# Another order of 950 TensorE units in a talking-heads attention with a squared-ReLU layer behind it

## The chip, the cores and the metric

One core of a Trainium2 chip runs the whole program. The metric is the device time of one execution in microseconds (us), less is better. Engines: TensorE (PE, with its weight loads PEld), VectorE (DVE), ScalarE (ACT), GpSimd (POOL) and SyncE (SP); the last two issue nearly all transfers.

## What is computed

Attention over 8 batches of 12 heads, 448 positions and 64 columns, in which the heads are mixed by two 12 x 12 matrices: once before the softmax and once after. Behind it comes a layer with 2048 hidden columns.

```python
scores = scale * np.matmul(q, k.transpose(0, 1, 3, 2))
scores = np.einsum('bhij,hg->bgij', scores, w_pre)
scores = scores - np.max(scores, axis=-1, keepdims=True)
attn = np.exp(scores)
attn = attn / (np.sum(attn, axis=-1, keepdims=True) + 1e-09)
attn = np.einsum('bhij,hg->bgij', attn, w_post)
return np.matmul(attn, v).astype(np.float32)
...
x = np.ascontiguousarray(attn_out.transpose(0, 2, 1, 3)).reshape(B * S, H * D)
h = np.maximum(x @ w_in, 0.0)
return (h * h @ w_out).astype(np.float32)
```

Inputs and output are float32; the kernel multiplies in bfloat16.

## The kernel before, in words

The kernel does not loop on the chip. Python code writes out one long program: it first records tasks (one engine, one function that emits instructions, the tasks it depends on), then a planner class, `_Plan`, puts them in an order for each engine, and then `emit_engine` (line 1405) emits each engine's tasks in that order, with semaphore waits for what they depend on. Each engine works strictly in its order, so whatever stands first and waits holds up all that is behind it.

A batch goes through these stages. TensorE's work is cut into *units*, each some 2 to 28 matmuls, and each kind of unit is a stream (the digit in brackets):

- **transposes** [0] (`emit_T`, line 711; matmuls at lines 731 and 735): q and k of a third of the heads, loaded by POOL into `qraw` and `kraw` (`load_qk`, 598), are transposed and copied into `qkt`. There are 6 units a batch, q and k for each third of the heads.
- **QK** [1] (`emit_QK`, 867; line 884): scores of a tile of up to 128 positions, copied by ACT or DVE into one half of `stage` (lines 450 and 451). A half is written again two tiles later.
- **ring moves** (`emit_rel`, 923): SP moves the scores from `stage` into the ring `dring` of 16 slots, so that 10 positions of all 12 heads (a *chunk*, 45 a batch) lie on the partitions of one slot. A slot is filled again when the pre unit 16 chunks earlier has read it.
- **pre** [2] (`emit_pre`, 945; line 953): two chunks of scores times the first mixing matrix. For each chunk ACT then takes the exponential, with the row sums (an *exp*, line 970), DVE the reciprocal (984), and POOL multiplies the second mixing matrix by it (a *fold*, 991).
- **direct** [5] (`emit_direct`, 822; line 832): in batch 0 alone the first 22 chunks are computed without `stage` and ring, from q scaled by the mixing weights.
- **post** [3] (`emit_post`, 1005; line 1023): 16 small matmuls that mix the heads of two chunks and transpose them; copied into `a2t`. A `pring` slot serves again 10 chunks later.
- **AV** [4] (`emit_AV`, 1066; line 1082): attention times v, copied into `xt`; two halves a batch.
- **F1** [6, 7] (`emit_F1`, 1118; lines 1128 and 1149): the first matrix of the layer, then ReLU (ACT or DVE, 1180 and 1181) and square (DVE, 1190) into `h2t`.
- **F2** [8, 9] (`emit_F2`, 1249; lines 1269 and, at the very end, 1218): the second matrix; results are copied to `osb` and sent out by POOL.

A unit writes into one or two of the 8 PSUM banks. It can begin only when the copies of an earlier unit out of these banks are done; these copies, called evacuations here, run on ACT or DVE, whichever the planner expects to finish earlier. Units come in four tilings of the array (full, two rows, two columns, quarters).

The order of TensorE's units is no result of the planner. It is written out by hand as a string of 950 digits, `ORDER` (line 28): each digit takes the next unit of that stream. All other engines' orders follow from it: the planner walks through the string with built-in estimates of each task's duration, of transfers and of instruction loading (in blocks of `BLOCK` = 256 instructions), and appends at each step the task that can start first. Tasks of loads and ring moves are so placed among POOL's folds and SP's queue. At the start of the program, up to `WARM`, it also fills expected idle time of TensorE with matmuls on dummy data (`warm_up`, 560; line 572).

```python
t = self.streams[int(order[at])][0]
if t.nwait:
    return None
est = max(self.free[PE], t.avail)
...
per_engine, committed = plan.run(ORDER)
```

Of the kernel before, what the change touches and what calls it, by code (L numbers as in the profile page):

```python
# [25 lines left out]
DMA_END = {"move": 2800.0, "load": 2300.0}  # L26
INF = float("inf")
ORDER = (
    "0000115551100515551555555555511555555531155333555555511355555555553335550022555533320000"
    "2434112411116333366622727737321622267711367373363111244422266663117723377613372166611227"  # L30
    "7722009333921193922380202821833830021441114218133822382183317613167222177633166336222444"
    "2236731267331761376111702028366228338338311777722002441226666333377220071811381118222893"
    "1193319131922291933392244344229163316220071173362216173337362216721761002637337002288111"
    "8331822291913393319222444223833181138113822244423161162273373163161227373202062263731736"
    "1163720027200291191139311932283281138133822244422391191339233922244422383383181138116331"
    "6020276227263721177337336216600226371172200933911191339222818111831382228183338324444224"
    "4228363161200733763226171171633622276376733372200441118822383182002931193319119223922293"
    "1913833831813811922244442216736227161367336117163372276221673373391229129393822283833382"
    "2244438222836883367676336736764447676766787877667667677879989988988999"
)  # L40


# [1418 lines left out]
```

## Time and profile before

| what | value |
|---|---|
| median of 3 runs | 526.93 us (525.52 to 529.73) |
| the profiled execution: time | 527.09 us |
| the profiled execution: span from first to last instruction | 525.3 us |
| TensorE busy | 514.3 us, 98% |
| ACT busy | 426.7 us, 81% |
| DVE busy | 394.1 us, 75% |
| POOL busy | 198.0 us, 38% |
| transfers issued by software queue q0, by q1 | 32.81 MB, 37.32 MB |
| read from HBM, written | 45.70 MB, 11.01 MB |

How to read it: busy time of TensorE counts a matmul from its start to a modelled end, and neighbours overlap, so 98% does not say that 2% is all that is lost. In the lists below a line such as `DVE stage L451` names an engine, the tile it writes and the line of the kernel; `x28` is a count of instructions. In a list of waits, the engine that waited stands left of the arrow, what ended the wait right of it; then total us, times, and the longest in us.

### The profile page before, as it was taken

How to read it: one execution, taken by the hardware profiler on the slowest of the kernel's cores; microseconds unless marked ns; L12 is line 12 of the kernel's file. 1: busy time of each engine (PE TensorE's matmuls, PEld its weight loads, DVE VectorE, ACT ScalarE, POOL GpSimd, SP SyncE). 2: the span in 40 equal slices, each digit the busy share in tenths (PEclk: the TensorE clock that was granted, in tenths of full speed). 3: DMA queues.
4: the chain of work that ended last, by engine and by line, in shares of the span. 5: the costliest groups of instructions: out<-in, count | busy, mean ns of one | idle time of the engine just before them, and what ended most of it. 6: DMA issues, size and time to landing. Idle time of an engine off the chain costs nothing.

```text
span 525.3 us, 23159 instructions
## 1 busy us (share of the span) xinstructions
PE 514.3 (98%) x9636; PEld 325.9 (62%) x9636; DVE 394.1 (75%) x987; ACT 426.7 (81%) x1221; POOL 198.0 (38%) x391
## 2 busy tenths in 40 slices
PE   8998999999999999999999999999999999999997
PEld 3455677567776564566547664577555665467874
DVE  8946988789979668878887787975788768865330
ACT  3879999889989889888998888988889877886321
POOL 9703445424641364134633456024632232242000
PEclk9999999999999999999999999999999999999999
DMA  8999999746984589636984699437963567541003
GB/s 160 204 216 181 170 170 189 182 105 143 179 168 87 128 173 183 138 75 154 177 167 93 150 180 181 102 71 153 198 122 82 124 142 131 114 105 45 3 20 101
DMA packets 82172, 71.79 MB, mean 137 GB/s; under 512 B 13222, under 2 KB 79446, under 8 KB 82070
## 3 DMA queue, kind: packets, MB, share of 16 engines
q0 software_dynamic: 36624, 32.81, 38.6%
q1 hardware_dynamic: 45158, 37.32, 29.3%
q8 instruction: 77, 1.26, 1.0%
q10 hardware_dynamic: 288, 0.20, 0.1%
q14 instruction: 25, 0.20, 0.1%
HBM read 45.70 MB, written 11.01 MB: 108 GB/s over the span
## 4 chain that ended last, share of the span: by engine, by line
PE 88%; DVE 4%; ACT 4%; DMA 2%; issue 1%; POOL 0%; DVEq 0%
PE ps L1269 26%; PE ps L1149 17%; PE ps L1023 8%; PE ps L953 7%; PE ps L1082 7%; PE ps L1128 7%; PE ps L884 6%; PE ps L832 5%; PE ps L1218 2%; PE ps L735 2%; ACT pring L970 2%; DMA dring<-stage 2%; ACT stage L450 1%; DVE stage L451 1%; PE ps L731 1%
## 5 line engine op out<-in xcount | busy, mean ns | idle before, releaser
L970 ACT ACTIVATE pring<-ps 128x448 bf16<-128x448 f32 x360 | 191.0, 555 | 14.3 <-PE ps L953 8.3
L1269 PE MATMUL ps<-w_out_sb,h2t 64*128 64x384 bf16 x1664 | 152.0, 323 | 0.1
L991 POOL TENSOR_TENSOR wk2s<-wk2b,rinv 128x120 bf16<-128x120 bf16 (+1 forms) x179 | 69.3, 392 | 210.8 <-DVE rinv L984 210.2
L451 DVE CAST a2t<-ps 128x480 bf16<-128x480 f32 (+1 forms) x194 | 118.1, 638 | 17.4 <-PE ps L1023 16.0
L1149 PE MATMUL ps<-xt,w_in_sb 64*128 64x448 bf16 (+2 forms) x1344 | 121.8, 323 | 0.2
L451 DVE CAST stage<-ps 128x448 bf16<-128x448 f32 (+1 forms) x174 | 104.3, 617 | 12.9 <-PE ps L884 10.0
L1269 PEld LDWEIGHTS ps<-w_out_sb,h2t 64*128 64x128 bf16 x1664 | 79.7, 94 | 49.8 <-issue 3.6
L450 ACT ACTIVATE stage<-ps 128x448 bf16<-128x448 f32 (+1 forms) x186 | 96.4, 557 | 17.2 <-PE ps L884 16.4
L450 ACT ACTIVATE a2t<-ps 128x480 bf16<-128x480 f32 (+1 forms) x174 | 92.3, 580 | 13.4 <-PE ps L1023 13.0
L1149 PEld LDWEIGHTS ps<-xt,w_in_sb 64*128 64x128 bf16 x1344 | 61.2, 94 | 41.2 <-PE ps L953 2.5
L970 ACT ACTIVATION_READ_ACCUMULATOR pring<-ps 128x1 f32 x360 | 79.4, 221 | 0.0
L1301 POOL DMA_DIRECT2D out_dram<-osb x52 | 33.6, 652 | 103.2 <-ACT pring L970 47.4
L1023 PEld LDWEIGHTS ps<-wk2s,pring 60*128 60x128 bf16 x2880 | 55.7, 93 | 23.7 <-issue 4.2
L1023 PE MATMUL ps<-wk2s,pring 60*128 60x60 bf16 x2880 | 61.7, 187 | 2.0 <-issue 0.9
L1190 DVE TENSOR_TENSOR h2t<-h1t 128x448 bf16<-128x448 bf16 (+2 forms) x176 | 52.6, 327 | 8.4 <-ACT h1t L1180 7.9
L984 DVE RECIPROCAL rinv<-rowsum 128x2 f32<-128x2 f32 (+1 forms) x184 | 28.9, 157 | 38.1 <-ACT pring L970 37.8
L1180 ACT ACTIVATE h1t<-ps 128x448 bf16<-128x448 f32 (+2 forms) x85 | 38.7, 462 | 20.0 <-PE ps L1149 16.8
L953 PE MATMUL ps<-dring,wk 60*64 60x448 bf16 (+1 forms) x676 | 52.2, 363 | 0.8 <-ACT pring L970 0.6
L1181 DVE TENSOR_SCALAR h1t<-ps 128x448 bf16<-128x448 f32 (+2 forms) x91 | 43.3, 485 | 11.9 <-PE ps L1149 7.8
L884 PE MATMUL ps<-qkt 64*128 64x448 bf16 (+1 forms) x360 | 49.2, 353 | 1.0 <-DVE h1t L1181 0.8
L1128 PE MATMUL ps<-xt,w_in_sb 128*128 128x228 bf16 (+1 forms) x384 | 42.2, 260 | 0.0
L1082 PE MATMUL ps<-a2t,vraw 128*64 128x220 bf16 (+1 forms) x768 | 40.7, 260 | 0.0
(57 smaller groups left out, 422.6 us busy)
## 6 DMA issues: line engine op xcount, KB each, us to landing
dring<-stage SPq DMA_DIRECT2D x309, 105.0 KB
out_dram<-osb POOLq DMA_DIRECT2D x52, 192.0 KB, 4.1
qraw<-in_q_dram POOLq DMA_DIRECT2D x42, 112.0 KB, 5.3
kraw<-in_k_dram POOLq DMA_DIRECT2D x42, 112.0 KB, 5.3
w_in_sb<-in_moe_w_in_dram POOLq DMA_DIRECT2D x8, 384.0 KB, 16.6
vraw<-in_v_dram POOLq DMA_DIRECT2D x24, 128.0 KB
w_out_sb<-in_moe_w_out_dram POOLq DMA_DIRECT2D x8, 384.0 KB, 8.4
vraw<-in_v_dram POOLq DMA_DIRECT2D x24, 96.0 KB
```

The costliest lines, as they stand in the source:

```text
L450: return eng.activation(o, i_, AF.Copy)
L451: return eng.tensor_copy(o, i_)
L884: r_ = eng.matmul(ps[y * w:(y + 1) * w, g.banks[x], 0:S], qkt[r0:r0 + 64, pb, p + y, 0, i0:i0 + w], qkt[r0:r0 + 64, pb, p + y, 1, :], star ...
L953: r_ = eng.matmul(ps[64 * y:64 * y + 64, gr.banks[x], 0:S], wk1[64 * x:64 * x + 64 - R0 * x, :], dring[64 * x:64 * x + 64 - R0 * x, (g0 + ...
L970: return eng.activation(pring[:, pr, 0:S], ps[:, gr.banks[x], 0:S], AF.Exp, accum_out=rowsum[:, pr, :])
L991: return eng.tensor_tensor(wk2s[:, p0:p0 + n, :], i0.to_broadcast([128, n, PR]), rinv[:, p0:p0 + n, :].to_broadcast([128, n, PR]), ALU.mult)
L1023: r_ = eng.matmul(ps[:, gr.banks[x], o0:o0 + PR], pring[64 * x:64 * x + PR, pr + y, j0:j0 + 2 * PJ], wk2s[64 * x:64 * x + PR, pr + y, :], ...
L1082: r_ = eng.matmul(ps[kk * 64:kk * 64 + 64, g.banks[0], x * n:(x + 1) * n], vraw[:, h, s, :], a2t[half][:, s, h, a0:a0 + n], start=(s == 0) ...
L1128: r_ = eng.matmul(ps[:, g.banks[0], 0:n], w_in_sb[:, ft, t * 128:(t + 1) * 128], xt[:, ft, c0:c1], start=(ft == 0), stop=(ft == NFT - 1))
L1149: r_ = eng.matmul(ps[:, g.banks[x], 0:n], w_in_sb[64 * y:64 * y + 64, ft, t * 128:(t + 1) * 128], xt[64 * y:64 * y + 64, ft, c0:c1], start ...
L1190: return eng.tensor_tensor(h2t[:, t16, o0:o0 + n], h1t[:, s, 0:n], h1t[:, s, 0:n], ALU.mult)
L1269: r_ = eng.matmul(ps[:, g.banks[hh], 0:FH], h2t[64 * y:64 * y + 64, t16, col:col + 128], w_out_sb[64 * y:64 * y + 64, t16, hh * FH:(hh + 1 ...
```

## The change

The string `ORDER` is replaced by another of the same length with the same count of each digit (48 zeros, 159 ones, 173 twos, 184 threes, 48 fours, 50 fives, 88 sixes and sevens, 64 eights, 48 nines). The new one is from a search that began at large steps in its first third and was cooled over the whole. Within a stream the units keep their order; how the streams interleave is new from the third digit on. All orders of the other engines that the planner derives are made anew with it, and so is which of ACT and DVE does an evacuation. No function is changed.

```diff
 ORDER = (
-    "0000115551100515551555555555511555555531155333555555511355555555553335550022555533320000"
-    "2434112411116333366622727737321622267711367373363111244422266663117723377613372166611227"
...
-    "1913833831813811922244442216736227161367336117163372276221673373391229129393822283833382"
-    "2244438222836883367676336736764447676766787877667667677879989988988999"
+    "0011005551150055551551555555555555555330055555111555555513355533155331552255555531333002"
+    "4310022434111663372217667223376262233773613177631114214422367672266733326731177112671136"
...
+    "1193393381833811182224442237631611736131617222763363622267127733739311922939222883338338"
+    "2224442228383383676768676776337674447676776767686866776978989988988999"
 )
```

In the two built programs each engine issues the same kinds of instructions: TensorE 9636 matmuls in both, in 956 and 957 units with the warm-ups (6 and 7 of them, 20 matmuls in both). The tiling changes 267 times between neighbouring units before and 269 times after. ACT's tasks go from 861 to 851, DVE's from 979 to 989. Batch 1's first two transposes (the seventh and eighth zero) come between the two halves of chunk 9's direct scores instead of behind those of chunk 19. SP's queue has the same order in both.

More of the change, by code (lines that the diff above doesn't have):

```diff
@@ L28 @@
 ORDER = (
-    "0000115551100515551555555555511555555531155333555555511355555555553335550022555533320000"
-    "2434112411116333366622727737321622267711367373363111244422266663117723377613372166611227"
[L31 to L37, printed above, removed]
-    "1913833831813811922244442216736227161367336117163372276221673373391229129393822283833382"
-    "2244438222836883367676336736764447676766787877667667677879989988988999"
+    "0011005551150055551551555555555555555330055555111555555513355533155331552255555531333002"
+    "4310022434111663372217667223376262233773613177631114214422367672266733326731177112671136"
+    "6702209323920209339121838122833820021441114218123833383118326112772226667133176333722442"
+    "2671336611142003772238316613627228338338122777620103442176633722002676711181318133822289"
+    "3319311931192224913392244422991161363371373611620027237362216721376100262733372020811813"
+    "3831182229193319313922244422381381118333822244422163361371237316116222737200263363372137"
+    "6211672007022091191339113922381183118133822244422293193319333922244314128318221836181363"
+    "3722762216730027336216712007363226171372200911931193319222838331811382228118333822444224"
+    "4431831613600271172267316376122673337371002763362244412288311820208239313922191193392229"
+    "1193393381833811182224442237631611736131617222763363622267127733739311922939222883338338"
+    "2224442228383383676768676776337674447676776767686866776978989988988999"
 )
```

## The prediction

> **What bounds the kernel now.** I read the head of the profile first, then the chain that ended last, then TensorE's waits, and last the timeline and the chain around its longest pauses.
>
> ```profile
> span 525.3 us, 23159 instructions
> PE 514.3 (98%) x9636; PEld 325.9 (62%) x9636; DVE 394.1 (75%) x987; ACT 426.7 (81%) x1221; POOL 198.0 (38%) x391
> PEclk9999999999999999999999999999999999999999
> ...
> PE 88%; DVE 4%; ACT 4%; DMA 2%; issue 1%; POOL 0%; DVEq 0%
> ```
>
> TensorE bounds: 98% busy, 88% of the chain, full clock in all slices. ACT and DVE, which empty PSUM, are at 81% and 75% and can hold it up in places. All that a new order can change is the pauses of TensorE. Busy time hides most of them (ends of matmuls are modelled), so I took steps: from the first matmul of a unit to the first matmul of the next. In the trace these are almost constant for one kind of unit. The lower quartile of each kind, in us: F2 1.30, F1 of 448 columns 1.14, AV 0.75 to 0.78, direct scores 0.57 or 0.38, transposes 0.22, post 0.22, pre and QK 0.19. A unit with a change of tiling behind it takes 0.09 to 0.10 more (F2 1.39, F1 1.23, post 0.32, pre 0.29).
>
> Summed over the 956 units, changes included: warm-up 8.6, transposes 13.6, QK 33.6, direct 25.8, post 42.8, pre 39.6, AV 38.8, F1 151.3, F2 148.2: 502.3 us. Measured from the first matmul to the last unit's end, the same stretch is 520.2. So **17.9 us are pauses**: 15 over 0.2 us make 7.2, 26 of 0.1 to 0.2 make 3.9, the rest are small. The five longest that have one cause show in the waits and pieces of the chain:
>
> ```profile
> PE ps L1023 <- issue: 0.9, 1, 0.9
> PE ps L884 <- DVE h1t L1181: 0.8, 1, 0.8
> PE ps L735 <- issue: 0.8, 1, 0.8
> PE ps L953 <- ACT pring L970: 0.6, 1, 0.6
> PE ps L1023 <- ACT stage L450: 0.5, 1, 0.5
> ```
>
> ```profile
> 47.51 0.43 PE L735 MATMUL ps<-ident,kraw 64*64 64x64 bf16 x28
> 47.82 0.41 PE L735 MATMUL ps<-ident,qraw 64*64 64x64 bf16 x28
> ...
> 50.77 0.37 PE L1023 MATMUL ps<-wk2s,pring 60*128 60x60 bf16 x14 [0.93 <-issue]
> ```
>
> ```profile
> 207.73 0.63 DVE stage L451
> ...
> 208.37 0.63 DVE stage L451
> ...
> 209.07 0.53 DVE stage L451
> ...
> 209.63 0.64 DVE h1t L1181
> ```
>
> Two are "issue" in the middle of a unit, after many tiny matmuls in a row (0.93 at 50 us; 0.75 at 373 us inside transposes). No semaphore is waited for there. The instruction queue q8 makes 77 transfers of 16 KB, each 0.9 to 1.8 long; TensorE's 19,272 matmuls and weight loads and some 960 waits over 77 is about 256 each, the planner's BLOCK. So I read these two as instructions that came late. The other three are surges of evacuations, as in the last fence: one engine works off four copies while TensorE has no free bank.
>
> **The change part by part.** Only the digits of ORDER differ. Side by side, both built kernels have 9636 matmuls and the same 950 units.
>
> *Steps without pauses.* Changes of tiling go from 267 to 269, warm-up matmuls stay 20 (in 7 runs, not 6). With the same steps the new order sums to 502.8: **+0.4**. One answer; nothing hides it, TensorE is the chain.
>
> *Surges.* I ran along each order with the steps above and kept a sum of evacuation asked for: 0.52 for an exp, 0.42 to 0.56 for copies, with 2 us of ACT and DVE taken off per us. In the old order, units at a sum over 2.5 us are 101, and lost some 38 ns each in the mean (0.93 at 50 us left out); units between 1 and 2.5 lost 19 to 24, below 1 us 7. In the new order the units over 2.5 are 81 (over 3.5: 6 for 12; highest 4.4 for 5.2), and 20 more lie below 1 us. Old losses on new counts: **-0.6**. Bounds: the three surges of 0.84, 0.65 and 0.52 gone and none for them, -2.0; as much anew, +2.0. I take -0.6, since the counts fall a little and nothing else does. Ten evacuations move from ACT (861 to 851 tasks) to DVE, the less busy one; they are in the counts.
>
> *Instructions.* Counted in blocks of 256, the densest block before takes 2.31 us of steps and is followed by the 0.93 pause; in the new order the densest there takes 3.26, because batch 1's first transposes move ahead by 15 us, between direct scores. That is 0.95 longer, as long as the pause: -0.9. What is late next there is a surge (sum 3.7 now, 4.6 before), counted above. The block at 373 us goes from 4.90 to 5.12: -0.2. But new blocks of 4.07 and 4.11 appear where the old ones of 4.22 to 4.35 cost 0 to 0.28: +0.2. **-0.9**; bounds -1.7 (both pauses gone) and +1.7 (two such new ones). [...]
>
> *Loads and the score ring.* POOL keeps its instructions, but its loads of q and k stand elsewhere among its folds, which wait for ACT and DVE. A place is the sum of the steps up to a unit; lead is the place of the transpose less the end of the last unit that anything ahead in POOL's queue waits for. The shortest before was 8.0 (batch 4, last k), then 9.2, and TensorE never lost 0.1 to one load after the start. Now it is 7.6 (batch 3, first k), 8.5, 8.9, 9.0 and 9.3.
>
> ```profile
> DMA to landing us min/median/max: 3.4/5.4/11.9
> ```
>
> At the median all are in time; at the maximum the first would cost 4.3. On SP's queue the moves of scores into the ring go out one per 0.8 to 1.2 us. Counted by 0.85 each and 4.2 to land, the tightest use of a ring slot has 2.1 us left (0.7 before), the tightest reuse of a stage half 1.9 (batch 7; 2.3 before). So **+0.4** for one load a little late; bounds 0 and +4.3. There are no gains here, since nothing here costs much now.
>
> *Post close behind pre.* The least way from a pre to its post grows tighter: 8 posts under 2.8 us, 2 before; 2.15 the shortest for 2.48. Behind lie two exps (2 x 0.52 and 0.22), a reciprocal of 0.16 and a fold of 0.39, some 1.9 with hand-overs. The old ones under 2.8 lost 0.01. **+0.2**; bounds 0 and 8 x 0.1.
>
> *The end.* Both orders end in the same 12 F2 units, so the last 5 us stay: 0.
>
> Sum: 0.4 - 0.6 - 0.9 + 0.4 + 0.2 = -0.5. The profiled execution took 527.1 (span 525.3 and 1.8 around it), 0.2 above the median of the runs, 526.9. So 526.6 for such an execution, **526.4** as a median.
>
> **Rivals.**
>
> *No different.* The planner sees neither late instructions nor late landings truly, so pauses might come back elsewhere: 17.9 again, 527.1 + 0.4 = 527.5 profiled, 527.3 as median. For it: surges of 3.1 us and more are 19 for 20 before. Against: the one block of 2.31 is gone for certain.
>
> *Slower: late loads.* Two or more of the five leads of 7.6 to 9.3 meet landings near 11.9. Transposes stand in TensorE's order, so all behind them waits. At the maximum the five cost 4.3 + 3.4 + 3.0 + 2.9 + 2.6; two of them 6 to 7.7: 533. It decides from a landing 9 us after the lead's start on. For it: landings at 78 to 102 us and 187 to 217 us run beside ring moves. Against: the old leads of 8.0 and 9.2 held.
>
> *Faster.* The surges and stalls over 0.2 us (7.2 us) go and none come: 526.9 + 0.4 - 7.2 = 520.1. For it: the highest sum falls by 0.8 us. Against: the number of surges hardly falls, and each order has its own.
>
> **How the numbers follow.** Forecast 0.50, no different 0.30, slower 0.11, faster 0.09. A measurement of this kernel can tell about 1% from no change (521.7 to 532.2): the first two cases lie within it, the others beyond. The forecast's own terms reach from 526.9 + 0.4 - 2.0 - 1.7 = 523.6 to 526.9 + 0.4 + 2.0 + 1.7 = 531.0 without a late load. The faster case lies half in; so the range is 521.8 to 531.0, with 0.1 above and 0.1 below left out. Faster 0.09, same 0.80, slower 0.11.
>
> **What would show it.** Right: no "issue" pause of over 0.5 us at TensorE near 50 us; TensorE's steps again sum to about 503; its pauses to 16 to 18. Surges: the waits of TensorE for ACT and DVE total less. Loads: no wait of line 735 for a transfer. Wrong: a wait for a transfer at batch 2 to 5's transposes (lines 735), or a pause of over 2 us at any one place.

## The result, and the profile after

| | before | changed |
|---|---|---|
| median of 20 runs each | 526.78 us (524.68 to 531.76) | 531.36 us (527.25 to 537.42) |
| the profiled execution: time, span | 527.1, 525.3 us | 531.7, 529.8 us |
| TensorE's steps | 502.3 us | 502.8 us |
| TensorE's pauses | 17.8 us | 21.9 us |

The ratio is 1.0062 (95% interval 1.0037 to 1.0088): some 3.3 us slower (4.6 by the medians), where a gain of 0.5 had been worked out. Runs over 1.5% above the fastest of their kernel are left out of the ratios as disturbed: 537.42 here, and in the experiments one run each of e3, e8 and e9, three of the twelve of e10 (531.55 to 532.44; with all runs counted its mean lies at 1.0010) and four of the kernel before.

The head of the profile and the engine line of the chain, which answer to the first lines shown of before:

```profile
span 529.8 us, 23188 instructions
PE 515.2 (97%) x9636; PEld 323.2 (61%) x9636; DVE 400.0 (76%) x997; ACT 421.6 (80%) x1211; POOL 198.5 (37%) x391
PEclk8999998999999999999999999999999999999999
...
PE 85%; DMA 5%; DVE 4%; ACT 3%; issue 1%; POOL 0%; SPq 0%; DVEq 0%; ACTq 0%
```

Busy times are nearly as before, but transfers went from 2% of the chain to 5%, and the granted clock fell below full speed in slices 1 and 7. What TensorE waited for (us in total, times, longest):

```profile
PE ps L735 <- issue: 2.5, 1, 2.5
PE ps L953 <- DMA dring<-stage: 1.9, 1, 1.9
...
PE ps L1023 <- POOL wk2s L991: 0.7, 2, 0.5
PE ps L735 <- DMA kraw<-in_k_dram: 0.5, 1, 0.5
```

Two lines are new in kind: TensorE waits for a move of scores into the ring (L953 is pre), and a little for a load of k. The pause of 0.93 at 50 us in a post is gone; at nearly the same place one of 2.49 stands in batch 1's transposes (start, duration, engine, line, idle before it):

```profile
51.93 0.41 PE L735 MATMUL ps<-ident,qraw 64*64 64x64 bf16 x28
54.84 0.41 PE L735 MATMUL ps<-ident,kraw 64*64 64x64 bf16 x28 [2.49 <-issue]
```

The chain shows the ring wait from the other side:

```profile
72.83 0.16 SPq L930
...
73.03 10.37 DMA dring<-stage
...
83.44 0.40 PE ps L953 x4
```

The tenth move of batch 1 left SP's queue at 73.0, took 10.4 us to land, and the pre that reads it began the moment it was there. Windows of 3 to 7 us show the clock (the last three columns are granted clock, DMA share and GB/s):

```profile
8.40:15.30 6.90, 6.18 (x89) 2.94 (x82) 6.24 (x18) 2.60 (x5) 6.90 (x13) 0.51 1.24 205
...
80.00:83.50 3.50, 1.14 (x16) 0.64 (x13) 1.19 (x6) 1.98 (x8) 3.31 (x7) 1.00 1.21 221
83.50:87.00 3.50, 3.50 (x22) 2.58 (x22) 1.40 (x6) 1.16 (x4) 0.98 (x2) 0.53 1.08 192
```

TensorE did 1.14 us of work between 80.0 and 83.5, and behind this it ran at half clock for 3.4 us. The same stretches before, at full clock:

```profile
8.40:15.30 6.90, 6.87 (x160) 3.96 (x161) 6.87 (x20) 3.27 (x8) 6.90 (x13) 1.00 1.25 205
...
83.50:87.00 3.50, 3.50 (x40) 2.31 (x38) 3.17 (x11) 3.26 (x10) 1.04 (x3) 1.00 0.94 151
```

Pauses summed by place (sum of the steps up to a unit, in us) say where the 4.0 more came from:

| place | 0–19 | 19–42 | 42–68 | 68–102 | 102–200 | 200–300 | 300–400 | 400 on |
|---|---|---|---|---|---|---|---|---|
| before | 1.05 | 0.22 | 2.84 | 2.10 | 3.85 | 3.25 | 3.67 | 0.86 |
| changed | 3.56 | 0.15 | 3.04 | 5.71 | 2.66 | 3.21 | 2.56 | 0.97 |

2.5 is the half clock at the start, 3.6 is the stretch with the ring wait and the half clock behind it, and 2.3 comes back between 102 and 400 us. One profile can hold accidents, so the experiments had to say which of these belongs to the order.

### The profile page after: what moved, and what is told of

It is laid out like the page before. It is cut to its first block, busy times and chain, and to the rows that moved or that the text cites. A ratio compares the mean times of both kernels' runs of the same rounds, so it can differ in the third digit from the quotient of the medians.

```text
span 529.8 us, 23188 instructions
## 1 busy us (share of the span) xinstructions
PE 515.2 (97%) x9636; PEld 323.2 (61%) x9636; DVE 400.0 (76%) x997; ACT 421.6 (80%) x1211; POOL 198.5 (37%) x391
## 4 chain that ended last, share of the span: by engine, by line
PE 85%; DMA 5%; DVE 4%; ACT 3%; issue 1%; POOL 0%; SPq 0%; DVEq 0%; ACTq 0%
PE ps L1269 25%; PE ps L1149 19%; PE ps L1023 7%; PE ps L953 7%; PE ps L1082 6%; PE ps L884 6%; PE ps L832 5%; PE ps L1128 5%; PE ps L1218 2%; DMA dring<-stage 2%; DMA kraw<-in_k_dram 2%; PE ps L735 2%; ACT pring L970 1%; DMA wall<-in_w_pre_dram 1%; ACT stage L450 1%
## 5 line engine op out<-in xcount | busy, mean ns | idle before, releaser
L451 DVE CAST a2t<-ps 128x480 bf16<-128x480 f32 (+1 forms) x194 | 118.9, 641 | 17.8 <-PE ps L1023 17.1
L451 DVE CAST stage<-ps 128x448 bf16<-128x448 f32 (+1 forms) x183 | 109.5, 617 | 14.5 <-PE ps L884 12.5
L1269 PEld LDWEIGHTS ps<-w_out_sb,h2t 64*128 64x128 bf16 x1664 | 78.2, 94 | 50.6 <-issue 2.2
L450 ACT ACTIVATE stage<-ps 128x448 bf16<-128x448 f32 (+1 forms) x177 | 90.8, 553 | 17.8 <-PE ps L884 17.2
L450 ACT ACTIVATE a2t<-ps 128x480 bf16<-128x480 f32 (+1 forms) x174 | 91.6, 572 | 15.4 <-PE ps L1023 15.0
L1181 DVE TENSOR_SCALAR h1t<-ps 128x448 bf16<-128x448 f32 (+2 forms) x93 | 45.4, 497 | 14.4 <-PE ps L1149 7.8
L953 PE MATMUL ps<-dring,wk 64*64 64x448 bf16 (+1 forms) x676 | 52.3, 361 | 3.0 <-DMA dring<-stage 1.9
L1180 ACT ACTIVATE h1t<-ps 128x448 bf16<-128x448 f32 (+2 forms) x83 | 36.7, 446 | 22.0 <-PE ps L1149 15.3
L884 PE MATMUL ps<-qkt 64*128 64x448 bf16 (+1 forms) x360 | 50.3, 357 | 0.8 <-DVE qkt L451 0.7
L1128 PE MATMUL ps<-xt,w_in_sb 128*128 128x220 bf16 (+1 forms) x384 | 43.5, 266 | 0.0
```

Source lines behind the costliest of these rows:

```text
L450: return eng.activation(o, i_, AF.Copy)
L451: return eng.tensor_copy(o, i_)
L884: r_ = eng.matmul(ps[y * w:(y + 1) * w, g.banks[x], 0:S], qkt[r0:r0 + 64, pb, p + y, 0, i0:i0 + w], qkt[r0:r0 + 64, pb, p + y, 1, :], star ...
L953: r_ = eng.matmul(ps[64 * y:64 * y + 64, gr.banks[x], 0:S], wk1[64 * x:64 * x + 64 - R0 * x, :], dring[64 * x:64 * x + 64 - R0 * x, (g0 + ...
L1128: r_ = eng.matmul(ps[:, g.banks[0], 0:n], w_in_sb[:, ft, t * 128:(t + 1) * 128], xt[:, ft, c0:c1], start=(ft == 0), stop=(ft == NFT - 1))
L1269: r_ = eng.matmul(ps[:, g.banks[hh], 0:FH], h2t[64 * y:64 * y + 64, t16, col:col + 128], w_out_sb[64 * y:64 * y + 64, t16, hh * FH:(hh + 1 ...
```

## The experiments

The theory to test: the ring wait costs the 3 us, and it comes from one digit. The last QK unit of batch 1's first tile stands at digit 108 of the new order and at 99 of the old (counted from 0; by steps, 53.6 against 49.9 us), and SP can begin the moves of this tile only when that unit's scores are copied out. The rivals: the half clock at the start, the pause near 50 us, or the new order behind 102 us. Ratios below are to runs of the kernel before on the same chip; they rest on 6 runs of e3, 9 of e5 and e7, and 12 of each of the others.

**Splices: which stretch holds the loss.** At digits 28, 78, 144 and 216 both orders have used up the same units, so pieces can be exchanged there. They lie at about 19, 42, 68 and 102 us of steps.

```diff
-ORDER = new
+ORDER = old[:28] + new[28:]                    # e1_old_start
+ORDER = new[:78] + old[78:144] + new[144:]     # e2_old_42_68
+ORDER = new[:144] + old[144:216] + new[216:]   # e3_old_68_102
+ORDER = old[:216] + new[216:]                  # e4_old_head
+ORDER = new[:216] + old[216:]                  # e5_new_head
```

> The new order with its first 28 digits replaced by the old ones (the first 28 hold the same units in both, up to about 19 us). In the profile of the new kernel TensorE's clock was granted at 5.0 us, fell to half at 8.5 and came back at 15.3; the old one had it from 9.8 on without a break. Theory: the start of the new order brings the fall, and it costs about 2 of the 4.5 us between the two spans. Then this kernel's profile has the full clock from about 10 us on without a break at the start, and takes 1.5 to 2.5 us less than the new one, some 529 where the new one has 531. Rival: the fall comes by chance of when the clock's windows lie, in either order; then there is no gain, 531.

> The new order with digits 78 to 143 (about 42 to 68 us of steps) replaced by the old ones; the stretch holds the same units in both. Theory: this stretch has the instruction pause of 2.5 us (0.9 in the old one) and it makes the ring moves of batch 1's first tile late (63 us for 56), which leads to the ring wait of 1.9 at 81 us and the half clock behind it (1.6). Then both are gone or small, and the kernel takes 3 to 5 less than the new one: about 527. Rival: only the instruction pause lies here, and the ring wait comes from the next stretch: 1.6 less, about 529.5. Second rival: the loss is spread thin over the whole order: 0.3 less.

> The new order with digits 144 to 215 (about 68 to 102 us of steps) replaced by the old ones. Theory: the ring wait at 81 us is made by late ring moves of the stretch before, so it stays here in some form, and the kernel takes 0 to 1.5 less than the new one: 529.5 to 531. Rival: the order within this stretch (v loads ahead of q loads in POOL's queue, pre units early) makes the wait: 3.5 less, 527.5.

> The old order up to digit 215 (102 us of steps), the new one from there on. Theory: the whole loss of the new kernel lies ahead of the cut (12.4 us of pauses there against 6.2), and behind it the new order is better (9.5 us of pauses against 11.7). Then this kernel is 1 to 3 us faster than the old one, 524 to 526, with a ratio below 1. Rival: the loss is spread over the whole order: halfway between the two, 529.

> The new order up to digit 215 (102 us of steps), the old one behind. Theory (the loss lies ahead of the cut): slower than the old kernel by as much as the new one or more, 3 to 5 us, ratio 1.006 to 1.010. Rival (spread over all): half of that, ratio 1.003.

| | median | ratio, 95% interval | pauses at 42–68 | at 68–102 |
|---|---|---|---|---|
| e1, old start | 531.32 us | 1.0073 (1.0039 to 1.0106) | 4.07 us | 4.18 us |
| e2, old from 42 to 68 | 528.97 | 1.0012 (0.9977 to 1.0046) | 4.60 | 1.56 |
| e3, old from 68 to 102 | 532.21 | 1.0113 (1.0051 to 1.0176) | 1.64 | 6.76 |
| e4, old up to 102 | 527.62 | 0.9985 (0.9951 to 1.0018) | 2.94 | 1.49 |
| e5, new up to 102 | 532.63 | 1.0085 (1.0054 to 1.0116) | 3.95 | 5.91 |

The head holds the loss (e5) and the tail neither loses nor gains what could be measured (e4, where a gain of 1 to 3 us had been expected). The start costs nothing on the mean: with the old one the loss stays (e1), though that profile had full clock throughout (1.00 granted on the mean). What matters most is that cause and pause lie in different stretches: the pauses are at 68 to 102, but giving that stretch its old digits doesn't help (e3 came out above the expected 529.5 to 531), while old digits at 42 to 68, where the late QK unit stands, do (e2). In e3, the wait has the same name as in the changed kernel and is longer:

```profile
PE ps L953 <- DMA dring<-stage: 3.2, 1, 3.2
...
PE ps L735 <- issue: 0.6, 1, 0.6
```

The "issue" pause is 0.6 here, and the loss is there all the same: the pause near 50 us isn't what the kernel lost by.

In e1 and e5 the ring wait is smaller, 0.7 and 1.1 us. There TensorE waited longer, 2.3 and 2.0 us in all, for the loads of batch 2's first q and k. The waits of e5:

```profile
PE ps L953 <- DMA dring<-stage: 1.1, 1, 1.1
PE ps L735 <- DMA kraw<-in_k_dram: 1.1, 1, 1.1
PE ps L735 <- DMA qraw<-in_q_dram: 1.0, 1, 1.0
```

So a late QK unit can cost by the ring alone or by the ring and these loads together. The two k loads left POOL at 82.6 and 83.6 us in e1 and landed in 7.2 and 11.3 us. In e6 below, which differs in the start and in that one digit, they left at 82.2 and 83.2, landed in 5.6 and 7.1, and nothing waited for them. What made them land later in e1 isn't tested.

**One digit.** In the new order this QK unit is moved ahead, and in the old one moved back; no other digit changes. The planner makes the other engines' orders anew from it, so one evacuation in e6 and 18 in e7 change between ACT and DVE; SP's order stays.

```diff
-"...43411166337221766..."     # e6_qk_early: new order, digit 108 to 101
+"...43411116633722766..."
-"...4111163333666227277..."   # e7_qk_late: old order, digit 99 to 110
+"...4111633336662271277..."
```

> The new order with one digit moved: the last QK unit of batch 1's first tile goes from digit 108 to 101, right behind its sister, as the old order has it. The ring moves of that tile can then start 3.5 us of steps earlier. By the reckoning with 4.2 us to land, pre units 46 to 54 have 8.3 to 10.0 us left for 5.4 to 7.1. Theory: the ring waits of TensorE between 68 and 84 us (1.9 and some half clock in the new kernel, 1.5 and 0.9 and 3.4 in the two others that keep its stretch from 42 to 68) come from this one digit: the profile has no ring wait over 0.5 us there, and the time is 2 to 3.5 less than the new kernel's, ratio 1.000 to 1.003. Rival: the waits come from other things in the stretch (loads of the second weight matrix in a bunch, instruction pauses): ratio stays at 1.005 to 1.007.

> The old order with one digit moved: the last QK unit of batch 1's first tile goes from digit 99 to 110, some 5 us of steps later, so that the ring moves of that tile start as late as in the new order or later; pre units 46 to 54 have 3.0 to 6.0 us left for 6.8 to 9.8. Theory: ring waits appear between 68 and 84 us, and the kernel is 2 to 4 us slower than the old one, ratio 1.004 to 1.008. Rival: 0 to 0.5 us, ratio 1.000.

e6: 527.25 us, ratio 0.9984 (0.9951 to 1.0017). e7: 533.07 us, 1.0095 (1.0057 to 1.0134). One digit gives the loss back in the new order and makes it in the old. Waits of e6, and then of e7:

```profile
PE ps L1023 <- issue: 1.7, 2, 1.3
...
PE ps L735 <- issue: 1.4, 1, 1.4
...
PE ps L731 <- DMA kraw<-in_k_dram: 0.4, 1, 0.4
```

```profile
PE ps L1023 <- issue: 2.8, 2, 2.3
PE ps L953 <- DMA dring<-stage: 2.6, 1, 2.6
```

The line of L953 for the ring is absent in e6 and there in e7, where the move that ended the wait, the eighth of batch 1, took 9.4 us. Pauses at 68 to 102: 1.78 in e6, 5.46 in e7.

**The landing.** A ring move of 105 KB that needs 10 us is slow for its size: the median of the changed kernel's 367 moves is 4.8 us. Beside it run the loads of w_out (8 of 384 KB). POOL issues them behind its folds, and the last four come together at 64 to 69 us, among the moves at 63 to 73 us (the changed kernel's POOL timeline):

```profile
58.31 0.78 POOL L664 DMA_DIRECT2D w_out_sb<-in_moe_w_out_dram  x1
...
64.39 1.54 POOL L664 DMA_DIRECT2D w_out_sb<-in_moe_w_out_dram  x2
...
67.44 1.54 POOL L664 DMA_DIRECT2D w_out_sb<-in_moe_w_out_dram  x2
```

e8 and e9 make these loads small, in the new and in the old order: 48 of each 384 columns are loaded, and the rest of the weight is left out. The order of every engine stays what it is without this edit.

```diff
-                                          [[F, 128], [128 * F, nt], [1, wc]])
-                            dst = w_out_sb[:, j * nt:(j + 1) * nt, x * wc:(x + 1) * wc]
+                                          [[F, 128], [128 * F, nt], [1, wc // 8]])
+                            dst = w_out_sb[:, j * nt:(j + 1) * nt, x * wc:x * wc + wc // 8]
```

e10, e11 and e12 load everything, but tie the eight loads to earlier units: e10 in the new order, e11 in that of e6, e12 in the old one.

```diff
-                            pre_at(min(24 + 3 * (2 * j + x), NCH - 1))]),
+                            pre_at(min(22 + 2 * (2 * j + x), NCH - 1))]),
```

> The new order; the loads of the second weight matrix bring 48 of each 384 columns (an eighth of the bytes), the rest of that matrix is left out, so the output is not the reference's. Theory: the ring moves land late (10.4 us for the usual 4) because they share the transfer engines with these loads at 64 to 76 us; without most of their bytes the ring waits at 68 to 84 us go even with the late start, and the instruction pause near 50 us shrinks below 1 us: 2.5 to 4.5 less than the new kernel, ratio 0.998 to 1.001. Rival: the moves are late by SP's queue alone: ring waits stay, ratio 1.004 or more.

> The old order with the w_out loads cut to 48 of each 384 columns (the rest of the weight is left out). If the loads cost only by delaying ring moves that TensorE waits for, the old order, whose moves stand ahead of their use by 6.8 us or more, gains 1 us or less: a ratio of 0.998 to 1.000 against 0.9963 for the new order with the same cut, and its pauses stay at 17 to 18 us. If the loads also delay other things in both orders (instructions, q and k loads), the old order gains as the new one did, 3 us or more: a ratio of 0.995 or lower, with the pause near 50 us shorter.

> The new order untouched, all of w_out loaded, but its eight loads are tied to pre 22, 24 ... 36 in place of 24, 27 ... 45, so they are issued before the ring moves of batch 1 and not beside them. If the late QK unit hurts only because its ring moves share the DMA engines with bunched loads, the wait for the ring at pre 54 goes and the time comes to 526 to 528 us, ratio 0.996 to 1.001, with ring moves at 72 us landing in 4 to 7 us. If the order is slow of itself (the moves are simply issued too late), it stays at 530.5 to 532, ratio 1.005 to 1.009. A third way: loads between 45 and 60 us delay instructions, and the pause near 50 us grows past 3 us.

> The new order with the QK digit moved ahead, and the w_out loads tied to pre 22 to 36. If both mend the same wait, the second adds nothing: 526.5 to 528, ratio 0.997 to 1.001, as with the digit alone. If the loads cost something of their own in the stretch of 42 to 68 us (that stretch lost 2.5 us less with small loads), bringing them forward moves that cost and makes the ratio 1.001 to 1.005, or takes it away and gives 0.993 to 0.997.

> The old order with the w_out loads tied to pre 22 to 36. Where the old order's ring moves have time enough, it changes by less than 0.2%: a ratio of 0.998 to 1.002. If sooner loads are a gain or a loss by themselves, this run shows it without the new order: beyond 0.4% either way.

In the table, "landing" is the tenth move of batch 1, from its issue on SP to the last event of its semaphore, and "spare" the time from there to the pre that reads it.

| | order | w_out | median | ratio, 95% interval | landing | spare | pauses at 68–102 |
|---|---|---|---|---|---|---|---|
| before | old | as it was | | | 8.5 us | 5.2 us | 2.10 us |
| changed | new | as it was | 531.36 us | 1.0062 (1.0037 to 1.0088) | 10.4 | 0.0 | 5.71 |
| e6 | new, QK early | as it was | 527.25 | 0.9984 (0.9951 to 1.0017) | 9.7 | 3.0 | 1.78 |
| e8 | new | small | 525.76 | 0.9963 (0.9930 to 0.9997) | 3.9 | 3.7 | 1.31 |
| e9 | old | small | 527.45 | 0.9987 (0.9953 to 1.0022) | 4.3 | 9.4 | 1.76 |
| e10 | new | sooner | 528.07 | 0.9992 (0.9952 to 1.0031) | 5.6 | 4.2 | 2.06 |
| e11 | new, QK early | sooner | 527.68 | 0.9993 (0.9958 to 1.0028) | 7.8 | 5.4 | 1.19 |
| e12 | old | sooner | 529.15 | 1.0022 (0.9978 to 1.0065) | 4.5 | 9.1 | 1.57 |

The new order untouched loses nothing once the loads don't run beside the moves: e10's interval lies wholly below that of the changed kernel. e8 says the same with the orders of all engines unchanged. So it takes both, a late QK unit and loads at the same time; mending either is enough, and mending both (e11) adds nothing. In the old order the same cut of the loads shortens the landing too (8.5 to 4.3) and changes nothing that can be told, since there were 5.2 us to spare. The windows from 72 to 76 us of the changed kernel and of e10 show the DMA engines:

```profile
72.00:76.00 4.00, 4.00 (x59) 2.76 (x58) 4.00 (x13) 3.91 (x11) 0.00 (x0) 1.00 1.17 211
```

```profile
72.00:76.00 4.00, 4.00 (x77) 2.84 (x72) 2.59 (x6) 3.77 (x11) 1.46 (x3) 1.00 0.32 89
```

They moved 211 GB/s in the first and 89 in the second, when the loads were already in. From 64 to 75 us the packets of POOL's queue q0 took 71.5% of the DMA engines' time in the changed kernel and those of SP's queue q1 24.7%; in e10 it was 27.9% and 39.8%. SP's tenth move landed in 10.4 us beside POOL's loads, in 3.9 beside the small ones (e8) and in 5.6 behind the sooner ones (e10).

e12 shows that sooner loads are no free gain. In its profile the old order's pause near 50 us, 0.93 before, was the longest of all profiles, with half the clock behind it (0.52 granted from 53.1 to 56.5 us):

```profile
49.69 0.20 PE L1023 MATMUL ps<-wk2s,pring 60*128 60x60 bf16 x2
53.55 0.54 PE L1023 MATMUL ps<-wk2s,pring 60*128 60x60 bf16 x14 [3.65 <-issue]
```

Over its 12 runs it is at 1.0022, which can't be told from no change. Nor did any version that computes everything beat the kernel before by what could be measured; e6 came nearest.

## Why the prediction was wrong, step by step

**Loads and the score ring (+0.4, bounds 0 and +4.3): this step failed.** Its 0.4 stood for one load a little late; what came was a late ring move, with half clock or late loads of q and k behind it, and the stretch from 68 to 102 us lost 3.6 us more than before. Three things were wrong in it. First, the price: 4.2 us for a move to land, whatever runs beside it. In the trace of before the median of the 367 moves was 4.8 us, and the tenth move of batch 1 took 8.5; the price that I needed was there, in the semaphore events of the very moves. Second, I looked for the tightest use of a ring slot in the whole order (2.1 us left, 0.7 before) and found it better. Batch 1 wasn't the tightest by that count: the pre that reads the tenth move had 9.8 us to spare in the old order and 5.4 in the new. But there the moves run beside the loads of w_out, which are issued at 39.9 to 64.1 us in before, at 43.0 to 68.2 in the changed kernel and nowhere else. With the landing as measured after, 5.4 + 4.2 − 10.4 = −0.8: a wait; with 8.5 as in before, 1.1 us would have been left, which is no cover. Third, I set the upper bound by a late load and not by a late ring move, and then left that bound out of the range. Both signs that the prediction listed as "wrong" came: a wait for a transfer at batch 2's transposes (0.5 us here, 2.3 and 2.0 in e1 and e5), and a pause of over 2 us at one place (2.49 us, near 52 us).

The place of the pause misled too: it lies at 72 us of steps, among digits that don't cause it. The cause is 19 us earlier in the order, in a QK unit that nothing on TensorE was late for.

**Instructions (−0.9): not borne out.** The reading of these pauses as late instructions holds. In the fourteen profiles TensorE has 42 "issue" pauses of 0.40 to 3.65 us behind the first 20 us, and each of them ended 1.2 to 1.6 us after a transfer of the instruction queue q8 had ended, though there are only 77 such transfers in a profile. The size doesn't hold. The pause of 0.93 in the post near 50 us went, as foreseen, but it came back in batch 1's transposes, at the same 47 us of steps. Over the profiles with that stretch in the new order it was 0.7 to 2.7 us (eight, middle value 0.8), with the stretch in the old one 0.4 to 4.0 (six, middle 1.2). In five of the eight (e1, e5, e6, e10 and e11) a second one, of 1.1 to 2.3 us, stands in a post 5 us of steps later, and in one of the six (e2, 1.5). Pauses over 42 to 68 us with full loads have a mean of 3.2 in the new (seven profiles, 1.6 to 4.1) and 4.4 in the old (five, 2.8 to 6.9). A gain of about 0.9 may lie in that scatter, but it isn't shown. Longer time for the densest block didn't remove its pause. The q8 transfers ahead of the 42 pauses took 0.9 to 1.4 us each; what varied is when they began. In e12, with its 3.65, the transfer began 1.2 us after TensorE had stopped. What holds it back is open. The profiles with small loads had 1.1 (e8, new order) and 2.9 (e9, old) there, so contention with loads may be part of it, in the new order at least; two single profiles don't settle it.

**Steps without pauses (+0.4): right.** 502.8, as worked out.

**Surges (−0.6) and the end (0): not to be told from nothing.** The new tail behind 102 us with the old head (e4) is at 0.9985, with an interval of 1.8 us either way around −0.8. What TensorE waited for ACT and DVE behind the start went from 1.9 us (0.8, 0.6 and 0.5) to 1.7 (0.7, 0.5 and 0.5).

**Post close behind pre (+0.2): about right.** Posts waited 0.7 us in all for POOL's fold, the last step from a pre to its post; before it was 0.4.

**What no step held: the clock.** The prediction took full clock as given. The half clock from 8.6 to 15.4 us cost 2.5 us in the profile after. But e6, e8 and e10 have the same start and ran at full clock from 5.4 to 5.8 us on, and the old start (e1) won nothing, so I count it as chance. Mean clocks below 0.997 are no matter of this start alone: 8 of the 20 runs of the changed kernel have one, and 20 of 93 of the kernel before (3 of 29, 8 of 29 and 9 of 35 in three sets). They are more frequent where the ring wait is: 28 of 56 runs of the changed kernel, e1, e3, e5 and e7, and 28 of 96 of the other experiments.

Of the sum without the ring the runs say: with the one digit moved ahead, the new order stands at 0.9984 (0.9951 to 1.0017) where the prediction's 526.4 for 526.9 is 0.9991. The rest of the sum agrees with this; it isn't proved by it, since the interval holds no change as well. The rival "slower: late loads" had the right kind of event (landings near 11 us that TensorE's order can't step around), but looked for it where the lead is shortest. The transfers that were late are the ring moves and, in the changed kernel, e1 and e5, batch 2's first q and k loads. In the changed kernel the four loads of these had 10.0 to 14.1 us from issue to use and took 7.3 to 12.9 to land, while the tightest load of all, with 5.3 us (batch 3, first k), landed in 3.9.

## What to carry to other kernels

For each transfer that a later instruction waits for, take the landing from that transfer's own events in that stretch of the trace, or from the slowest neighbour, and compare it with its own slack; a minimum of slack over the whole run with a mean landing finds the wrong place. When an order of work changes, follow the unit that releases a chain of transfers, not only the units that wait for them: here a unit moved by nine digits cost 3 us, 19 us of work later. And ask what the other queues move at that time: without those loads the same lateness cost nothing that could be measured.

## What the runs showed of the hardware

The granted clock changed on a grid of 3.41 us. In the clock records of all fourteen profiles every stretch but the last lasts a whole multiple of it; in the changed kernel they are 3.41 us at full clock, 6.83 at half, 68.27 at full, 3.41 at half and 443.73 at full. The falls went with how little TensorE worked, by its busy time, within one step of the grid. Of 2099 steps at full clock up to the end of its work, seven had less than 1.9 us of TensorE's work (0.05 to 1.79), and six of them were followed by half clock; none of the others was. The one exception is a step of the changed kernel at 53.0 us, with 1.54.

So in these profiles the place of a wait on the grid mattered as well as its length. In the changed kernel half clock ran from 83.7 to 87.1, behind waits of 0.5 and 1.9 us at two pre units, which left 1.05 us of work in one step. In e3 it followed one wait of 3.2, with 1.0 us of work in the step:

```profile
78.60:82.00 3.40, 3.40 (x21) 2.54 (x18) 2.13 (x8) 0.72 (x4) 1.37 (x3) 0.52 1.12 191
```

In e7 it did not follow one of 2.6 at nearly the same place, which lay across two steps with 2.3 and 2.0 us of work:

```profile
79.50:83.00 3.50, 3.50 (x49) 2.74 (x50) 2.29 (x9) 1.46 (x5) 1.94 (x5) 1.00 1.29 215
```

The start shows the same: the step from 5.2 us of the changed kernel had 1.79 us of work, and with the same start in e2, e6, e8 and e10, where the step began 0.3 to 0.9 us later, it had 2.2 and no half clock followed.

At half clock 21 matmuls ran in 3.4 us (e3, 0.52 granted), at full clock 49 in 3.5 (e7, 1.00; not the same mix). The fall at 83.7 us of the changed kernel did not follow an idle step: no single pause before it reached 2.1 us, and the step had 1.05 us of work. The half clock there added about half as much again to the ring wait: in the profile after, the pauses before two pre units took 2.6 by steps and the units up to 87 us another 1.6.
